# A hand-ordered gated-recurrence and feed-forward kernel: a new order, chunk 3 transposed by DMA, the last output tile in halves

## The chip, the cores and the metric

The kernel runs on one core of a Trainium2 chip. The metric is the device time of one execution in microseconds (us), and the verdict compares medians of repeated runs. Beside the times there is one profiled execution, whose trace says for each instruction when it ran and what it had waited for. The engines are named as in the profile: PE (TensorE: matmuls; its weight loads are PEld), DVE (VectorE), ACT (ScalarE), POOL (GpSimd) and SP (SyncE, which here only issues DMAs).

## The reference

Two layers are computed one after the other. The first is a gated recurrence over 768 steps, for 4 batches and 8 heads of width 48:

```
f = 1 / (1 + exp(-f_logit))
for t in range(S):
    state = f[:, :, t, :, None] * state + einsum('bhd,bhde->bhde', k[:, :, t], v[:, :, t])
    y[:, :, t] = einsum('bhd,bhde->bhe', q[:, :, t], state)
```

Its output, as 3072 tokens of width 384 (8 heads by 48), goes through a feed-forward layer with 2048 hidden columns:

```
h = x @ w_in
g = h + sin(alpha * h)**2 / (alpha + 1e-9)
out = g @ w_out
```

Inputs and output are float32. The kernel does its matmuls in bfloat16.

## The kernel before

**Tiling.** The 768 steps are cut into 6 chunks of 128. In a chunk the recurrence becomes matmuls. Cumulative sums of the logarithm of f come from a matmul with a triangular mask (line 311), and ACT turns them into the factors `G` and `Gi`. DVE or POOL multiply q and k by these into a tile `qk` (line 329). The tile is transposed into `tr`, so that a 128x128 product of k and q can be made for each head (`a_`, line 368). DVE applies the triangular mask (line 372), and two sets of matmuls, with the carried state (`inter_`, line 378) and with v (`intra_`, line 384), give the chunk's y. The state for the next chunk is made by `kv_` (lines 400 and 402) and a multiplication (line 413). `attend(c, b)` does this for one chunk and one batch, 24 times in all.

**Two ways to transpose.** For chunks below `PE_TR` the tile `qk` is transposed by PE: eight matmuls with the identity into a PSUM bank (line 361, two steps of four), and one copy of 1024 columns to SBUF (line 421) on DVE or ACT. For the others SP issues one DMA transpose (line 424). Likewise y becomes the feed-forward's input `xT` by PE (line 392) and a copy (line 395) for chunks below `Y_TR`, and by a DMA transpose (line 440) for the others. `PE_TR` is 4 and `Y_TR` is 3.

**Feed-forward.** In `first` (line 474; `first_half`, line 493, for chunk 0) PE multiplies two 128-column blocks of `w_in` by a chunk's 512 tokens. ACT takes the sine (line 459), and DVE adds it to h (line 462) into `g`. `second` does one tile of 128 tokens by 384 output columns: 16 accumulating matmuls (line 506, in eight steps of two), one copy from PSUM (line 512) and one store of 192 KB (line 515). Both weight matrices are loaded as float32 in pieces of 768 KB (lines 251 and 271) and scaled by alpha into bfloat16 (lines 257, 276 and 278). The scale for `w_in` is spread over the partitions by PE in float32 (line 254).

**The order.** Every step is an `op` with the engines that may do it, a cost for each, and the steps it depends on. The costs play no part when the program is built: what decides is the list `ORDER`, which was planned beforehand. Each entry is a number that packs three things: the step (`x % 2000`), the engine among those allowed (`x // 2000 % 5`), and the PSUM bank (`x // 10000`).

```
for nth, x in enumerate(ORDER):
    o = ops[x % 2000]
    ...
    yield o, list(o.engs)[x // 2000 % 5]
```

Each engine runs its own instructions strictly in the order of this list. SP too: a DMA whose data are not ready keeps back all the DMAs behind it. The SBUF buffers of each kind (`SLOTS`) are handed out in the same order.

Of the kernel before, what the change touches and what calls it, by code (L numbers as in the profile page):

```python
# [18 lines left out]
ORDER = [6, 133, 134, 0, 2, 10136, 70, 137, 7, 20142, 139, 138, 143, 145, 144, 8, 2147, 3, 30050, 71, 10079, 81,  # L19
    40148, 20160, 1, 146, 161, 73, 80, 140, 149, 2084, 82, 74, 4, 162, 75, 60163, 2083, 20097, 76, 164, 10, 9,  # L20
    5, 98, 2150, 2077, 151, 99, 196, 40085, 14, 60100, 197, 86, 20199, 152, 2087, 101, 2135, 170, 2078, 50205,
    10153, 154, 51, 171, 40165, 2141, 2072, 60088, 155, 57, 166, 200, 201, 2204, 20107, 206, 207, 156, 10102,
    103, 54, 2167, 89, 40168, 50090, 237, 2157, 91, 60095, 12, 238, 70158, 104, 169, 108, 10056, 40105, 2092,
    2106, 240, 20246, 241, 50093, 2094, 159, 242, 247, 52, 70053, 30172, 58, 2210, 2209, 173, 96, 40112, 113,
    2203, 55, 174, 50187, 109, 10059, 114, 60, 60118, 188, 11, 248, 2251, 70184, 30175, 176, 15, 189, 202, 119,
    40121, 208, 185, 20115, 50181, 61, 177, 120, 10211, 16, 62, 212, 110, 30178, 60224, 225, 186, 17, 64, 70190,
    249, 116, 2213, 2250, 122, 111, 214, 191, 117, 182, 243, 226, 66, 20265, 266, 215, 2244, 60130, 2267, 183,
    252, 2239, 2063, 123, 68, 192, 10124, 40268, 18, 269, 253, 20127, 70193, 40270, 125, 271, 179, 22, 50748,
    254, 272, 126, 768, 273, 2065, 749, 769, 10758, 759, 245, 13, 40738, 739, 180, 30274, 131, 770, 67, 771,
    740, 760, 761, 762, 275, 763, 772, 128, 129, 69, 773, 132, 194, 2198, 20227, 195, 741, 742, 743, 764, 19,  # L30
    750, 228, 744, 745, 310, 765, 60255, 774, 20, 311, 26, 751, 20319, 25, 353, 354, 2766, 320, 746, 747, 30362,
    752, 775, 363, 40216, 217, 256, 10356, 322, 218, 60257, 219, 70229, 230, 753, 776, 231, 21, 321, 2323, 258,
    259, 2324, 20276, 277, 358, 40220, 357, 2260, 23, 232, 10313, 2312, 754, 755, 364, 261, 60235, 221, 24,
    70233, 262, 20339, 30222, 33, 2355, 234, 236, 27, 314, 756, 315, 428, 40263, 290, 291, 60294, 264, 340, 757,
    223, 359, 429, 318, 295, 40286, 287, 341, 292, 365, 296, 20278, 30, 279, 28, 293, 297, 282, 288, 283, 289,
    280, 60298, 284, 2360, 281, 299, 285, 300, 40306, 307, 20302, 303, 788, 10379, 789, 790, 791, 792, 301, 308,
    304, 309, 2367, 469, 60798, 799, 2366, 70382, 34, 40431, 433, 383, 305, 2317, 32, 50437, 20342, 380, 384,
    2361, 343, 800, 316, 438, 10368, 369, 370, 793, 794, 70393, 795, 432, 381, 40325, 439, 42, 2471, 801, 470,
    394, 31, 2796, 20385, 50344, 797, 37, 38, 434, 2436, 345, 10478, 395, 2442, 2435, 346, 326, 480, 479, 386,
    70778, 2347, 472, 473, 474, 779, 20371, 542, 440, 327, 29, 780, 802, 803, 2441, 40328, 767, 10443, 444, 373,  # L40
    372, 329, 543, 20330, 35, 2476, 804, 445, 781, 482, 30336, 374, 375, 2376, 40387, 41, 805, 2806, 807, 337,
    331, 332, 50350, 36, 10456, 545, 457, 388, 2333, 546, 389, 60377, 351, 390, 20446, 447, 782, 481, 483, 378,
    475, 46, 783, 784, 2458, 50507, 40808, 809, 547, 10551, 497, 498, 20459, 352, 60484, 2544, 485, 648, 785,
    810, 579, 508, 338, 2430, 460, 2499, 50334, 811, 812, 20500, 649, 486, 461, 2786, 2335, 462, 553, 813, 501,
    60448, 552, 463, 2464, 449, 70391, 40, 450, 50348, 814, 20487, 10502, 503, 349, 815, 2392, 451, 554, 50466,
    489, 43, 504, 580, 488, 60408, 787, 409, 2505, 816, 548, 777, 467, 509, 555, 490, 550, 20400, 2477, 410,
    40424, 491, 492, 401, 425, 411, 396, 397, 60404, 402, 405, 426, 403, 427, 398, 20416, 2549, 417, 493, 406,
    399, 40412, 413, 420, 421, 418, 407, 60828, 829, 830, 831, 568, 419, 414, 422, 415, 70838, 20656, 423, 452,
    506, 39, 30588, 40453, 50582, 590, 589, 454, 657, 592, 839, 840, 677, 841, 583, 658, 465, 832, 569, 833,
    842, 570, 468, 30494, 495, 843, 40571, 44, 2593, 817, 844, 845, 455, 846, 522, 584, 572, 573, 2496, 20514,  # L50
    515, 557, 847, 516, 523, 50848, 574, 47, 659, 70565, 849, 850, 2591, 586, 524, 851, 2585, 566, 517, 678,
    40576, 2581, 2660, 2587, 852, 853, 854, 834, 70651, 525, 855, 653, 2655, 835, 20818, 856, 2836, 30680, 558,
    594, 2556, 577, 681, 652, 819, 682, 820, 821, 822, 40595, 605, 60685, 70560, 559, 561, 562, 563, 686, 823,
    824, 567, 2654, 596, 825, 687, 48, 2689, 2826, 837, 606, 607, 45, 564, 60530, 531, 532, 20518, 519, 40510,
    511, 608, 688, 669, 609, 698, 610, 10597, 533, 520, 521, 857, 512, 598, 49, 2611, 599, 513, 2600, 601,
    60526, 527, 528, 575, 20613, 30602, 614, 538, 539, 529, 2650, 578, 540, 603, 40858, 859, 615, 50868, 869,
    870, 60534, 535, 871, 683, 872, 873, 661, 541, 860, 861, 2684, 2679, 20699, 878, 879, 536, 537, 880, 881,
    690, 612, 882, 883, 60670, 884, 885, 2886, 874, 10701, 700, 862, 702, 703, 604, 875, 20662, 671, 60620, 827,
    876, 2704, 691, 692, 50672, 673, 674, 863, 621, 2675, 622, 864, 663, 705, 865, 623, 50693, 616, 617, 676,
    694, 618, 695, 20632, 60664, 665, 2866, 696, 633, 70888, 889, 634, 619, 635, 40624, 625, 626, 644, 645, 890,  # L60
    891, 646, 20628, 627, 629, 647, 892, 40636, 666, 630, 697, 893, 894, 867, 2667, 895, 637, 898, 899, 631,
    10918, 638, 20640, 919, 668, 896, 639, 920, 641, 642, 643, 60706, 40714, 715, 900, 901, 902, 877, 20710,
    903, 904, 711, 905, 716, 717, 921, 922, 906, 923, 924, 925, 897, 712, 907, 713, 40718, 707, 908, 2926, 909,
    719, 20730, 708, 720, 910, 911, 709, 731, 10928, 721, 929, 930, 931, 932, 933, 934, 935, 936, 937, 60968,
    732, 733, 969, 970, 40722, 723, 724, 971, 725, 70958, 20726, 727, 887, 927, 728, 912, 913, 914, 40734, 959,
    960, 735, 729, 736, 737, 915, 10938, 20948, 949, 961, 2916, 950, 951, 952, 953, 954, 955, 956, 957, 972,
# [42 lines left out]
def kernel(  # L109
# [66 lines left out]
    def at(b):  # L176
        return T[b.ring][b.place]
# [166 lines left out]
    def attend(c, b):  # L344
# [84 lines left out]
        if not first:  # L429
            last_ = op({PE: 170}, inter_, deps=[a, made["st", c - 1, b]], takes=[yb], holds=[trb, sold])  # L430
# [149 lines left out]
```

## Time and profile before

| | |
|---|---|
| median of 4 runs | 194.16 us (193.87 to 194.5) |
| the profiled execution's own time | 194.26 us |
| its span, first to last instruction | 192.5 us |
| PE busy | 178.9 us (93%), 1545 matmuls |
| PE weight loads | 106.7 us (55%) |
| DVE busy | 135.8 us (71%) |
| ACT busy | 125.8 us (65%) |
| POOL busy | 63.7 us (33%) |
| mean granted PE clock | 0.952 of full speed |
| HBM read and written | 25.18 MB and 4.72 MB |

The span is 1.8 us shorter than the profiled execution's time; the rest lies before the first and after the last instruction. The busy time of PE counts a matmul from its start to its modelled end, and neighbouring matmuls overlap. How long one really occupies the array is read from the distance between the starts of neighbours. The row PEclk of the page gives the clock that the throttle granted in each fortieth of the span.

### The profile page before, as it was taken

To read this page: it belongs to the slowest core of one execution; us is meant where nothing else is said; L and a number is where in the kernel's file an instruction comes from. 1 tells how busy PE (TensorE), PEld (TensorE's weight loads), DVE (VectorE), ACT (ScalarE), POOL (GpSimd) and SP (SyncE) were. 2 spreads that over 40 slices of the span, in tenths; PEclk is the share of its full clock that TensorE was granted. 3 is DMA by queue.
4 is the path that set the end of the run, shared out by engine and by line. 5 is a ranking of instruction groups with operands and counts; after the bars stand their busy time and mean duration, and the time that the engine had idled before them with its cause. 6 is when DMAs were issued, how large, how long until landed. Compare 5 with 4: busy or idle time off the path is not lost.

```text
span 192.5 us, 3900 instructions
## 1 busy us (share of the span) xinstructions
PE 178.9 (93%) x1545; PEld 106.7 (55%) x1545; DVE 135.8 (71%) x171; ACT 125.8 (65%) x184; POOL 63.7 (33%) x92
## 2 busy tenths in 40 slices
PE   0687999999999899999989999999999999999992
PEld 0254746787567446677744555555555454555561
DVE  3067796599977699889889979789549764455420
ACT  2957775799787979778887888686225554442401
POOL 4277204760014295886560071565300000000000
PEclk9997555999999999999999999999999999999998
DMA  6999999989999999999999689968711130103023
GB/s 134 223 218 217 309 301 277 251 202 327 251 205 209 230 224 240 181 252 200 252 197 219 138 189 206 227 130 181 151 43 25 58 95 11 41 0 123 3 82 123
DMA packets 119732, 33.43 MB, mean 174 GB/s; under 512 B 113041, under 2 KB 118177, under 8 KB 119713
## 3 DMA queue, kind: packets, MB, share of 16 engines
q1 hardware_dynamic: 119680, 33.17, 80.2%
q8 instruction: 12, 0.20, 0.4%
q14 instruction: 6, 0.05, 0.1%
q10 hardware_dynamic: 34, 0.02, 0.0%
HBM read 25.18 MB, written 4.72 MB: 155 GB/s over the span
## 4 chain that ended last, share of the span: by engine, by line
PE 74%; DMA 11%; SPq 6%; DVE 3%; ACT 3%; issue 1%; POOL 0%; ACTq 0%; DVEq 0%
PE banks L506 29%; PE banks L474 24%; PE banks L493 6%; SPq L219 6%; DMA f<-in_f_logit_dram 3%; DMA v<-in_v_dram 3%; PE banks L254 3%; PE banks L368 3%; DMA out_dram<-osb 3%; DMA q<-in_q_dram 3%; PE banks L384 2%; PE banks L311 2%; PE banks L402 2%; PE banks L378 1%; PE banks L361 1%
## 5 line engine op out<-in xcount | busy, mean ns | idle before, releaser
L506 PE MATMUL banks<-w_out_bf,g 128*128 128x384 bf16 x384 | 72.4, 326 | 0.0
L462 DVE SCALAR_TENSOR_TENSOR g<-s,banks 128x1024 bf16<-128x1024 f32 (+1 forms) x56 | 57.9, 1063 | 16.9 <-ACT s L459 16.8
L459 ACT ACTIVATE s<-banks 128x1024 f32<-128x1024 f32 (+1 forms) x56 | 49.4, 903 | 31.1 <-PE banks L474 27.2
L474 PE MATMUL banks<-xT,w_in_bf 128*128 128x512 bf16 x240 | 57.1, 379 | 1.2 <-DVE yn L388 0.6
L506 PEld LDWEIGHTS <-g 128*128 128x128 bf16 x384 | 35.0, 98 | 23.0
L474 PEld LDWEIGHTS <-w_in_bf 128*128 128x128 bf16 x240 | 22.6, 98 | 25.0 <-issue 1.7
L372 DVE TENSOR_TENSOR at<-banks,mask 128x1024 bf16<-128x1024 f32 x24 | 29.1, 1221 | 6.3 <-PE banks L368 4.6
L329 POOL TENSOR_TENSOR qk<-q,G 128x384 bf16<-128x384 f32 x18 | 18.3, 1022 | 19.3 <-DMA q<-in_q_dram 13.3
L329 POOL TENSOR_TENSOR qk<-k,Gi 128x384 bf16<-128x384 f32 x21 | 21.1, 1016 | 9.8 <-DMA k<-in_k_dram 7.5
L297 POOL CAST vb<-v 128x768 bf16<-128x768 f32 x12 | 9.8, 823 | 23.8 <-DMA v<-in_v_dram 23.8
L290 ACT ACTIVATE f<-f 128x768 f32<-128x768 f32 x12 | 10.2, 848 | 7.0 <-DMA f<-in_f_logit_dram 6.9
L548 ACT ACT_TABLE_LOAD x11 | 14.1, 1283 | 0.2
L493 PE MATMUL banks<-xT,w_in_bf 128*128 128x256 bf16 x96 | 14.2, 309 | 0.0
L512 DVE COPY osb<-banks 128x384 f32<-128x384 f32 x12 | 6.7, 555 | 10.2 <-PE banks L506 7.8
L512 ACT COPY osb<-banks 128x384 f32<-128x384 f32 x12 | 5.7, 475 | 12.4 <-PE banks L506 12.4
L361 PE MATMUL banks<-ident,qk 128*128 128x128 bf16 x128 | 12.0, 233 | 2.0 <-POOL qk L329 1.8
L319 ACT ACTIVATE G<-banks 128x388 f32<-128x388 f32 (+1 forms) x24 | 11.8, 499 | 2.7 <-PE banks L314 1.9
L322 ACT ACTIVATE Gi<-banks 128x384 f32<-128x384 f32 x24 | 11.4, 492 | 2.3 <-PE banks L311 1.1
L493 PEld LDWEIGHTS <-w_in_bf 128*128 128x128 bf16 x96 | 10.2, 110 | 4.5 <-DVE w_in_bf L257 1.5
L413 POOL TENSOR_TENSOR st<-sum,gl 128x384 bf16<-128x384 f32 x11 | 9.4, 858 | 5.5 <-DVE sum L410 5.5
L311 PE MATMUL banks<-lf,mask 128*128 128x384 bf16 x24 | 8.9, 383 | 2.2 <-ACT lf L293 2.2
L361 PEld LDWEIGHTS <-qk 128*128 128x128 bf16 x128 | 8.5, 103 | 4.2 <-POOL qk L329 2.6
(55 smaller groups left out, 175.5 us busy)
## 6 DMA issues: line engine op xcount, KB each, us to landing
f<-in_f_logit_dram SPq DMA_DIRECT2D x12, 384.0 KB, 5.8
k<-in_k_dram SPq DMA_DIRECT2D x12, 384.0 KB, 5.4
q<-in_q_dram SPq DMA_DIRECT2D x12, 384.0 KB, 5.6
v<-in_v_dram SPq DMA_DIRECT2D x12, 384.0 KB, 5.8
out_dram<-osb SPq DMA_DIRECT2D x24, 192.0 KB, 2.1
wst<-in_moe_w_in_dram SPq DMA_DIRECT2D x4, 768.0 KB, 7.2
wst<-in_moe_w_out_dram SPq DMA_DIRECT2D x4, 768.0 KB, 6.8
xT<-yn SPq DMA_TRANSPOSE x12, 2.4
```

The source lines that it names most:

```text
L311: nc.tensor.matmul(cs[:, :H * D].rearrange("c (p r d) -> c p r d", r=2, d=D), mask, at(lf)[:, :, i, :, :D], start=True, stop=True)
L319: nc.scalar.activation(out=at(Gb)[:, :n_G], in_=ps(cb, n_G), func=Act.Exp, scale=-1.0)
L329: engine[e].tensor_mul(at(qkb)[:, j, :, :, :D], at(src)[:, i * H:(i + 1) * H, :].rearrange("c (r p) d -> c p r d", r=2), g.rearrange("c (p ...
L361: nc.tensor.transpose(ps(tpb, 1024, BF16)[:, (j * HP + p) * C:(j * HP + p + 1) * C], at(qkb)[:, j, p, :, :].rearrange("c r e -> c (r e)"), ...
L372: nc.vector.tensor_mul(at(atb), ps(ab, 1024).rearrange("c (r p t) -> c r p t", r=2, p=HP), mask4.unsqueeze(1).to_broadcast([C, 2, HP, C]))
L459: nc.scalar.activation(out=at(sb)[:, :n], in_=ps(hb, n), func=Act.Sin, bias=QUARTER)
L462: nc.vector.scalar_tensor_tensor(take(at(gb)), at(sb)[:, :n].rearrange("p (j t) -> p j t", j=2), -1.0, ps(hb, n).rearrange("p (j t) -> p j ...
L474: nc.tensor.matmul(ps(hb, 2 * TOK)[:, j * TOK:(j + 1) * TOK], w_in_bf[:, kb, f * P:(f + 1) * P], at(xb)[:, :, kb, :], start=(kb == 0), sto ...
L493: nc.tensor.matmul(h[:, j, :], w_in_bf[:, kb, (fb + j) * P:(fb + j + 1) * P], at(xb)[:, ts, kb, :], start=(kb == 0), stop=(kb == KB - 1))
L506: nc.tensor.matmul(ps(ob, d_model), at(bufs["g", c, fb])[:, j - fb, t * P:(t + 1) * P], w_out_bf[:, j, :], start=(j == 0), stop=(j == FB - 1))
L512: (nc.scalar.copy if e == ACT else nc.vector.tensor_copy)(at(sbuf), ps(ob, d_model))
L548: nc.scalar.preload_act_table_set(now)
```

## The change

Four things are changed.

1. `ORDER` is another list: all engines run the same kinds of steps in another order, partly on other engines and in other PSUM banks.
2. `PE_TR` goes from 4 to 3, so that the four `qk` tiles of chunk 3 are transposed by DMA.
3. `second` splits the very last tile (chunk 5, batch 3) into two halves of 192 output columns. Each has its own accumulation, copy and store. The new function `columns` holds what `second` held.
4. Costs in the `op` calls are altered (for instance 310 to 225 for `a_`, 2050 to 2500 for a weight load, 1700 to 1400 and 1000 to 500 for the DMA transposes). They describe what the new list was planned with; no instruction depends on them.

```diff
-ORDER = [6, 133, 134, 0, 2, 10136, 70, 137, 7, 20142, 139, 138, 143, 145, 144, 8, 2147, 3, 30050, 71, 10079, 81,
...
+ORDER = [2, 70, 71, 60073, 70079, 6, 40000, 133, 80, 74, 1, 3, 2082, 81, 4, 2076, 50059, 134, 70136, 75, 137,
...
-PE_TR, Y_TR, SUM = 4, 3, 2
+PE_TR, Y_TR, SUM = 3, 3, 2
...
-        l = op({SP: 500}, ld, takes=[b], dma=2050)
+        l = op({SP: 500}, ld, takes=[b], dma=2500)
...
-        a = op({PE: 310}, a_, deps=[tr], takes=[ab], holds=[trb])
+        a = op({PE: 225}, a_, deps=[tr], takes=[ab], holds=[trb])
...
     def second(c, t):
+        last = (c, t) == (NCH - 1, B - 1)
+        for ms in [slice(0, d_model // 2), slice(d_model // 2, d_model)] if last else [slice(0, d_model)]:
+            columns(c, t, ms, ms.stop - ms.start)
+
+    def columns(c, t, ms, n):
         ob, sbuf = Buf("ps"), Buf("osb")
         prev = None
         for fb in range(0, FB, 2):
             def mm(e, fb=fb):
                 for j in (fb, fb + 1):
-                    nc.tensor.matmul(ps(ob, d_model), at(bufs["g", c, fb])[:, j - fb, t * P:(t + 1) * P], w_out_bf[:, j, :],
+                    nc.tensor.matmul(ps(ob, n), at(bufs["g", c, fb])[:, j - fb, t * P:(t + 1) * P], w_out_bf[:, j, ms],
                                      start=(j == 0), stop=(j == FB - 1))
...
-            (nc.scalar.copy if e == ACT else nc.vector.tensor_copy)(at(sbuf), ps(ob, d_model))
+            (nc.scalar.copy if e == ACT else nc.vector.tensor_copy)(at(sbuf)[:, :n], ps(ob, n))
...
-            nc.sync.dma_start(out=out[t * S + c * C:t * S + (c + 1) * C, :], in_=at(sbuf))
+            nc.sync.dma_start(out=out[t * S + c * C:t * S + (c + 1) * C, ms], in_=at(sbuf)[:, :n])
```

## The prediction

> **What bounds the kernel now.** I read the page's busy times and slices first, then the table of stretches, then PE's timeline, then the chain.
>
> ```profile
> PE 178.9 (93%) x1545; PEld 106.7 (55%) x1545; DVE 135.8 (71%) x171; ACT 125.8 (65%) x184; POOL 63.7 (33%) x92
> ...
> PE   0687999999999899999989999999999999999992
> ...
> PEclk9997555999999999999999999999999999999998
> ```
>
> PE is the full engine, and its granted clock is half for three slices and part of a fourth. The table of stretches (PE, PEld, DVE, ACT and POOL busy, then clock, DMA share, GB/s) gives the edges:
>
> ```profile
> 17.10:34.20 17.10, 16.52 (x118) 10.11 (x117) 12.97 (x15) 11.93 (x22) 4.24 (x8) 0.50 1.09 284
> 34.20:46.40 12.20, 11.86 (x132) 9.59 (x131) 10.23 (x14) 10.98 (x19) 6.78 (x8) 1.00 1.01 267
> 46.40:102.00 55.60, 54.44 (x596) 34.14 (x595) 47.37 (x64) 45.73 (x70) 28.74 (x36) 1.00 1.14 222
> 102.00:142.00 40.00, 40.00 (x329) 22.06 (x328) 33.23 (x38) 27.16 (x37) 14.75 (x18) 1.00 0.82 171
> 142.00:189.20 47.20, 47.14 (x299) 25.43 (x298) 25.43 (x25) 19.26 (x23) 0.00 (x0) 1.00 0.16 51
> ```
>
> From 34.2 to 189.2 PE is idle for about 1.6 us in all (12.20-11.86, 55.60-54.44, 47.20-47.14). So the end is set by three things: how much PE has to stream, how long it streams at half clock, and about 3.3 us of tail after its last matmul. The tail is in the chain: the copy starts at 189.22 and takes 0.48; the span ends at 192.5.
>
> PE's timeline (start, duration) shows the half clock and what a change of form costs:
>
> ```profile
> 26.23 2.07 PE L254 MATMUL banks<-al_row,ones_f 1*128 1x512 f32 x2
> 28.23 5.30 PE L493 MATMUL banks<-xT,w_in_bf 128*128 128x256 bf16 x24
> 33.46 1.47 PE L254 MATMUL banks<-al_row,ones_f 1*128 1x512 f32 x2
> 34.86 4.10 PE L493 MATMUL banks<-xT,w_in_bf 128*128 128x256 bf16 x36
> ...
> 51.70 0.49 PE L506 MATMUL banks<-w_out_bf,g 128*128 128x384 bf16 x2
> 52.12 0.40 PE L368 MATMUL banks<-tr 64*128 64x128 bf16 x8
> 52.45 2.77 PE L506 MATMUL banks<-w_out_bf,g 128*128 128x384 bf16 x16
> ```
>
> 24 matmuls of line 493 need 5.23 us at half clock, 36 need about 4.0 at full: 0.218 against 0.11 each. Line 368 uses 64 rows of the array, its neighbours 128. The second L506 starts at 51.86 and should occupy 0.16, to 52.02; L368 starts at 52.12, so going in costs 0.10. Its eight starts lie (0.40-0.216)/7 = 0.026 apart (0.216 is one of them alone), which makes 0.21; L506 follows after 0.33, so going out costs 0.12. One run of L368 among others thus costs about 0.2 us beyond its own streaming.
>
> **What the Trainium skill says.** "TensorE: Matmul & The Clock Gate", section "What's actually happening": the clock is set by activity in free-running windows of 3.413 us, and returns to full after a busy window. The trace agrees on the length: 17.1 us at half clock are five windows. They end at 27.4, 30.8 and 34.2, and the one from 27.4, three quarters of it dense L493, was not enough. Section "Back-to-back issue gap": N/2.4 + 2.5 ns at full clock. Agrees: L506 (N=384) takes 0.163, as 32 of them fill 5.21 us of the chain. "DMA: Bandwidth & Descriptors", section "Issuing engines are not separate DMA queues": all DMAs share 16 engines and interleave. The list of DMA issues (last number: median us from issue to landing) agrees: loads, mostly issued while the engines were full, take longer than the eight `tr` transposes, which ran from 103 to 139:
>
> ```profile
> f<-in_f_logit_dram SPq DMA_DIRECT2D x12, 384.0 KB, 5.8
> ...
> tr<-qk SPq DMA_TRANSPOSE x8, 3.2
> ```
>
> **The change part by part.**
>
> *Chunk 3 by DMA.* Four tiles of eight L361 matmuls go. The chain has eight in 0.45 us, 0.056 each: 32 x 0.056 = -1.8 us of PE, in stretches where PE never rests, so on the path. Three DVE copies (0.685) and one ACT copy (1.007) go too. Added are four transposes on SP: 1.25 us of SP's time each (the eight of before: median 1258 ns), 5 us in all, and 3.1 to 4.1 us from issue to landing. In the new order they stand near together on SP, with one load between, ahead of f, k and v loads for the next chunk; these wait behind them if a `qk` is late. The bounds: nothing, if PE reaches `a_` later than the landing, to 5.8 - 3.2 = 2.6 us per wait if transposes in the crowded stretch land as late as loads.
>
> *Fewer changes of form.* The order of PE's instructions has the 192 L368 in 24 runs before and 17 after; chunk 0's four stay separate in both. 7 x 0.2 = -1.4 us, on the path. Bounds 1.3 and 1.6.
>
> *The start.* The first 17 DMAs on SP are the same but for one exchange: f of the fourth half-chunk now goes ahead of v of the second, which so lands some 1.8 us later than its 19.1, at about 20.9, and its cast ends near 21.7. PE has a 2.0 us L254, two L311 and others between, and reaches that v only near 23: hidden; with no cover it costs 1.8. Then comes the gain. Before, PE did an L254 (26.23 to 28.23) between the last y transpose and the first L493. After, L493 follows at once, needing `w_in_bf`, whose first fold ran 24.16 to 25.9 on DVE, and x. PE gets there near 26.4, still cold, and then has 24 L493 in a row, to 31.6. The window 27.4 to 30.8 is then dense throughout, and the clock should rise at 30.8, not 34.2: 3.41 x 1/2 = -1.7 us. With windows elsewhere in phase the dense 5.2 us still covers most of one, so -0.5 to -2.5; 0 if DVE keeps PE from using it. DVE is the cover that may be missing. Its row, with 1.75 a fold and 0.6 a sum (line 462): second fold to 28.5, three sums from 29.2, third fold once its L254 is through (32.3) to 34.0, a fourth sum, fourth fold to 36.3, six sums and an `st` to 40.4, the first `w_out` fold to 42.1, a sum to 42.7. PE's first L506 needs the last two: about 43, against 46.39. I take -1.6. A check: before, 142.8 us passed from the first L506 to the last matmul's end; counts times spacings give 1.3 less of PE work behind that point after, and with the 0.7 below the last matmul ends at 43 + 142.8 - 1.3 + 0.7 = 185.2, 4.0 earlier.
>
> *The last tile in halves.* 32 matmuls of 192 columns at (192/2.4 + 2.5) = 82.5 ns for 16 at 162.5: +0.05. The last copy is 192 columns: ACT takes 0.475 for 384 and 0.602 for 512, so 0.32 for 192: -0.15. The store is 96 KB for 192 KB. The last one before ran from 189.72 to its landing at 191.58; half the bytes save 0 to 0.35, I take 0.2. Sum -0.3.
>
> *Work moved between engines.* The order gives DVE 3 more `gl` (0.48), 2 more `qk` products (0.7), 3 more `st` (0.55) and 2 more `yn` (0.55), one `xT` less (0.35) and the 3 copies less: +3.2 us. ACT loses 1.3, POOL 5.5. DVE is busy 80.6 of the 95.6 us from 46.4 to 142, and 83.8 would still fit under PE. Without that cover it costs up to 3.2.
>
> *New waits.* Before has 1.6 us of PE idleness from 34.2 on, which the new order needn't repeat or keep. I take the same and 0.7 more, for DMA transposes and loads in the crowded stretch: bounds -1.2 and +8.
>
> Sum: -1.8 - 1.4 - 1.6 - 0.3 + 0.7 = -4.4. The profiled execution took 194.26 us (span 192.5), so 189.9; it lies 0.1 above the median of 194.16, hence 189.8. No difference under about 0.2% (0.4 us) can be told from no change.
>
> **The rivals.**
>
> *A. Part of it is given back.* PE's savings of 3.2 and the tail stand, but the clock rises in the same window as before, or DVE's 3.2 us come into the open, or a load is late. For: DVE and ACT are 85% and 82% busy in 46 to 102, and in the chain of before they and DMA waits appear between 83 and 101. Against: PE was idle for only 1.2 us there. With no gain at the start and 1.5 us of new waits: 194.2 - 3.5 + 1.5 = 192.2.
>
> *B. Slower: SP's queue.* The place is chunk 3, where PE reaches three of the four `a_` within 0.7 us of its own work and the fourth 4.5 us later. If the transposes land like loads, at 5.8 and not 3.2, PE stands twice for 2.6, and the loads for chunk 4 are issued 5 us later, a further wait of up to 5 when they are needed: +10. For: the stretch's DMA share is full, and a load of f from 83.52 that took 6.63 us and a q of 4.82 at 93.63 are links of the chain. Against: from 102 to 142 twenty transposes shared the queue with loads and PE was busy for 40.00 of 40.00. It decides once waits exceed 5.1 us; at 6.5 the time is 195.6.
>
> *C. The change does nothing to be seen.* That needs the waits to match 5.1 by chance.
>
> **How the numbers follow.** The forecast as summed 0.56, A 0.26, B 0.14, C 0.04. Forecast and A are faster: 0.82; same 0.04; slower 0.14. The forecast's own range is 188 to 191.3: the start at -2.5 and no new wait gives 188.2, the start at 0 gives 191.4. The range reaches over A: 187.8 to 193.8, with B and little else outside.
>
> **What would show it.** Right: 96 L361; the half-clock stretch ending at least one window earlier; the first L506 near 43; PE idle under 2.5 us from there to its end; the last matmul near 185; 3.0 us behind it. Wrong: PE waiting at line 368 for `tr` by DMA, or at line 474 or 493 for DVE; loads of chunk 4 late behind line 424's DMAs; or a half clock up to 34 us and beyond.

## The result: a little slower, and where the time went

The kernel after the change takes 195.08 us (median of 33 runs, 193.23 to 197.88), beside 194.25 us for the kernel before (54 runs). The ratio is 1.0031, 95% interval 1.0011 to 1.005. The forecast was 189.8. Medians here are of all executions, while the ratios leave out those more than 1.5% above the fastest of the same kernel, so a ratio can lie below that of the medians. The profiled execution of the changed kernel took 196.73 us (span 195.0), 1.6 us above its own median, so its losses are somewhat larger than those of a typical one. The lines after 500 have moved by five: line 506 is now 511, line 512 is 517, line 515 is 520.

The page of the kernel after, busy times and slices:

```profile
PE 176.3 (90%) x1529; PEld 106.5 (55%) x1529; DVE 139.2 (71%) x177; ACT 124.5 (64%) x183; POOL 59.7 (31%) x84
...
PE   0676989988999999999999929999999999999993
...
PEclk9996559999999999999999985999999999999998
DMA  6999999979899999899999939959895320100222
```

PE is busy 2.6 us less (178.9 before), and the half clock of the start ends a slice earlier. But in slice 24 of the 40 PE is 20% busy, and in slices 24 and 25 of its clock row (8 and 5) a second stretch of half clock stands, which the kernel before does not have. The table of stretches (columns as in the prediction) puts edges to it:

```profile
16.47:30.12 13.65, 12.29 (x111) 8.20 (x109) 10.10 (x13) 9.69 (x17) 2.24 (x5) 0.50 1.04 272
30.12:44.45 14.33, 13.08 (x115) 9.91 (x113) 12.65 (x15) 11.77 (x19) 7.91 (x8) 1.00 1.01 268
44.45:113.20 68.75, 68.51 (x709) 42.34 (x708) 60.38 (x77) 58.09 (x89) 29.08 (x38) 1.00 1.04 214
113.20:117.20 4.00, 0.09 (x4) 0.07 (x2) 0.84 (x2) 0.91 (x1) 1.78 (x2) 0.78 0.25 50
117.20:142.00 24.80, 24.80 (x187) 13.04 (x188) 18.07 (x20) 13.15 (x19) 11.40 (x13) 0.90 0.95 189
142.00:191.65 49.65, 49.41 (x345) 28.27 (x344) 28.92 (x31) 20.86 (x25) 2.48 (x3) 1.00 0.27 74
```

Between 44.45 and 113.2 us PE rests for 0.24 us; then it stands for four. PE's timeline names what it waited for (the bracket holds the idle time and what ended it):

```profile
26.81 4.38 PE L493 MATMUL banks<-xT,w_in_bf 128*128 128x256 bf16 x24 [0.41 <-ACT xT L395]
...
44.45 1.14 PE L511 MATMUL banks<-w_out_bf,g 128*128 128x384 bf16 x6 [0.95 <-DVE g L462]
...
112.99 0.26 PE L384 MATMUL banks<-vb,at 128*128 128x48 bf16 x4
117.16 1.44 PE L474 MATMUL banks<-xT,w_in_bf 128*128 128x512 bf16 x3 [3.91 <-DMA xT<-yn]
```

It is the first matmul of chunk 3's feed-forward, waiting for that chunk's y, which line 440 transposes by DMA. The clock records show half clock from 115.46 to 122.28, two windows; the 5.12 us of it in which PE worked cost 2.56. By the distance of the starts, less what the matmul before needs, the wait is 4.07 us; wait and clock together are 6.6 us. From there the balance closes. The first line-511 matmul starts 1.94 us earlier than before (44.45 for 46.39), what lies behind the last matmul's start is 0.39 shorter (3.34 for 3.73), and what lies between grows by 4.78 (147.20 for 142.42). The sum is the 2.5 us by which the span grew. Of the 4.78, +6.6 are wait and clock. The rest is -1.8: by the two tables of stretches, some 0.7 of it is short idleness of before that did not recur (1.2 us between 46.4 and 189.2 before, 0.5 between 44.45 and 191.65 now, the long wait apart), and some 1.1 is PE's lighter work.

Why the y transposes were late is read from two timelines of the kernel after. ACT makes the first of chunk 3's four y tiles:

```profile
102.75 0.48 ACT L388 CAST yn<-banks 128x384 bf16<-128x384 f32 x1 [0.41 <-PE banks L384]
```

SP issues its DMAs in the same stretch:

```profile
101.91 2.97 SPq L219 DMA_DIRECT2D v<-in_v_dram  x1
104.96 1.45 SPq L520 DMA_DIRECT2D out_dram<-osb  x1
106.51 1.26 SPq L424 DMA_TRANSPOSE tr<-qk  x1
107.82 0.57 SPq L219 DMA_DIRECT2D q<-in_q_dram  x1
108.44 7.53 SPq L440 DMA_TRANSPOSE xT<-yn  x4
```

The first y was ready at 103.23, and its transpose was issued at 108.44: a load of v held for 2.97 us, a store, a transpose of chunk 4 and a load of q stood ahead of it. The last of the four y's was ready at 107.64 and its transpose issued at 114.73; it landed at 117.07, 0.09 us before PE went on. In the kernel before, the same four were issued from 102.21 to 108.26 and had landed by 111.79, for a need at 113.82:

```profile
102.21 1.40 SPq L440 DMA_TRANSPOSE xT<-yn  x1
...
105.02 2.56 SPq L440 DMA_TRANSPOSE xT<-yn  x2
...
108.26 2.06 SPq L440 DMA_TRANSPOSE xT<-yn  x1
```

But they did not stand shorter in SP's queue there. The first and the last y of chunk 3 in the kernel before, and the last in the kernel after, are made here:

```profile
94.14 0.48 ACT L388 CAST yn<-banks 128x384 bf16<-128x384 f32 x1
100.57 0.55 DVE L388 CAST yn<-banks 128x384 bf16<-128x384 f32 x1
...
107.17 0.47 ACT L388 CAST yn<-banks 128x384 bf16<-128x384 f32 x1
```

From ready to issue, the first y took 7.6 us before and 5.2 after, the last 7.1 in both. What differs is when the y's are made. The new list puts chunk 2's 48 matmuls of line 474 (from 84.81 us) ahead of chunk 3's `a_` (from 98.19); in the kernel before these `a_` (from 87.45) came ahead of that block (from 96.28). PE was hardly idle up to 113.2 us, so this is the list and not a delay. The last y is ready 6.5 us later than before, for a need that comes 0.6 us earlier. From the last y to PE's need the old list has 12.7 us and the new one 5.6. Standing in the queue and landing took 10.7 us before and 9.4 after: it fits into the first and not into the second.

SP is behind in the loads too. By 100 us it has issued 42 loads of q, k, v and f before, and 38 after (with four transposes more); the last of the 48 lands at 134.16 before, at 143.07 after.

### The profile page after: what moved, and what is told of

Its sections match the earlier page's. It is cut to its first block, busy times and chain, and to the rows that moved or that the text cites. A ratio compares the mean times of both kernels' runs of the same rounds, so it can differ in the third digit from the quotient of the medians.

```text
span 195.0 us, 3886 instructions
## 1 busy us (share of the span) xinstructions
PE 176.3 (90%) x1529; PEld 106.5 (55%) x1529; DVE 139.2 (71%) x177; ACT 124.5 (64%) x183; POOL 59.7 (31%) x84
## 3 DMA queue, kind: packets, MB, share of 16 engines
q1 hardware_dynamic: 124048, 34.22, 80.3%
## 4 chain that ended last, share of the span: by engine, by line
PE 76%; SPq 7%; DMA 7%; DVE 4%; ACT 3%; issue 2%; POOL 0%; DVEq 0%
PE banks L511 31%; PE banks L474 25%; SPq L219 5%; PE banks L493 5%; PE banks L368 3%; PE banks L384 3%; DMA v<-in_v_dram 3%; DMA out_dram<-osb 3%; PE banks L254 2%; PE banks L311 2%; PE banks L378 2%; DVE g L462 2%; PE banks L402 2%; DVE w_out_bf L278 1%; SPq L440 1%
## 5 line engine op out<-in xcount | busy, mean ns | idle before, releaser
L511 PE MATMUL banks<-w_out_bf,g 128*128 128x384 bf16 (+1 forms) x400 | 72.5, 320 | 1.0 <-DVE g L462 1.0
L474 PE MATMUL banks<-xT,w_in_bf 128*128 128x512 bf16 x240 | 57.7, 389 | 4.4 <-DMA xT<-yn 3.9
L511 PEld LDWEIGHTS <-g 128*128 128x128 bf16 x400 | 35.9, 98 | 22.2 <-issue 1.7
L329 POOL TENSOR_TENSOR qk<-q,G 128x384 bf16<-128x384 f32 x19 | 19.0, 1006 | 37.1 <-ACT G L319 16.6
L329 POOL TENSOR_TENSOR qk<-k,Gi 128x384 bf16<-128x384 f32 x18 | 18.1, 1017 | 11.2 <-DMA k<-in_k_dram 10.5
L517 ACT COPY osb<-banks 128x384 f32<-128x384 f32 (+1 forms) x13 | 5.9, 456 | 16.8 <-PE banks L511 15.1
L493 PE MATMUL banks<-xT,w_in_bf 128*128 128x256 bf16 x96 | 13.1, 296 | 0.7 <-ACT xT L395 0.4
L388 DVE CAST yn<-banks 128x384 bf16<-128x384 f32 x13 | 7.1, 554 | 6.7 <-PE banks L384 6.7
L384 PE MATMUL banks<-vb,at 128*128 128x48 bf16 x192 | 10.8, 189 | 0.7 <-POOL vb L297 0.7
L384 PEld LDWEIGHTS <-at 128*128 128x128 bf16 x192 | 9.0, 101 | 3.2 <-issue 1.6
```

The lines of the kernel that those rows point to most:

```text
L329: engine[e].tensor_mul(at(qkb)[:, j, :, :, :D], at(src)[:, i * H:(i + 1) * H, :].rearrange("c (r p) d -> c p r d", r=2), g.rearrange("c (p ...
L384: nc.tensor.matmul(ps(yb, H * D)[:, h * D:(h + 1) * D], at(atb)[:, r, p, :], at(vb)[:, i, h, :], start=(first and p == r == 0), stop=(r == ...
L474: nc.tensor.matmul(ps(hb, 2 * TOK)[:, j * TOK:(j + 1) * TOK], w_in_bf[:, kb, f * P:(f + 1) * P], at(xb)[:, :, kb, :], start=(kb == 0), sto ...
L493: nc.tensor.matmul(h[:, j, :], w_in_bf[:, kb, (fb + j) * P:(fb + j + 1) * P], at(xb)[:, ts, kb, :], start=(kb == 0), stop=(kb == KB - 1))
L511: nc.tensor.matmul(ps(ob, n), at(bufs["g", c, fb])[:, j - fb, t * P:(t + 1) * P], w_out_bf[:, j, ms], start=(j == 0), stop=(j == FB - 1))
L517: (nc.scalar.copy if e == ACT else nc.vector.tensor_copy)(at(sbuf)[:, :n], ps(ob, n))
```

## The experiments

The first question was whether that one wait is the loss. **Theory 1** says yes: take it away, and the time falls to about 190. (Theory 2, in two of the expectations, says that other limits stand right behind it.) It fell, and **theory 3** took its place: the stream of loads, stores and transposes through SP and the 16 DMA engines is a second limit close behind PE's. (From 80 to 130 us these engines are busy 0.86 or more of every 10 us in the kernel before, and 0.96 or more in the kernel after but for the 10 us with the wait.) Whatever PE gains, it spends in waiting for the next item of that stream, and the four new transposes make the stream longer. Every ratio below is to the kernel before, run beside it on the same chip.

### The kernel after, once more

No edit.

> The changed kernel unaltered, for a second trace and as the yardstick of this call. If the profiled execution was typical, PE waits 3 to 5 us before its first line-474 matmul of chunk 3 for the DMA transposes of y, and the time is 194.5 to 195.6 us; if that wait was an accident of one execution, it is under 1 us here and the time is the same all the same.

195.22 us (22 runs), ratio 1.0024 [0.9995, 1.0053]. Its profile has the same wait (4.11 us, from 113.64) and the same two windows of half clock (116.12 to 122.94); but this execution took 197.87 us, 2.65 above the median, so no profile shows a typical execution. For those there are the recorded mean clocks of 56 executions of this kernel. In 36 it is 0.991, which is one window of 3.41 us at half clock in some 190 us, in 9 about 0.98, two windows, in 5 it is 1.0. In this profile, and in seven others of the new order, the record of the clock begins at 26 to 32 us, behind the half clock of the start, so that such figures leave it out. The mean does not say where the window lies, and the kernel before has 0.991 too (15 of 59 executions beside this run). But in the four kernels below that have the same start and a much shorter wait, 0.991 stands in 1 of 37 executions. So a later half clock most likely belongs to most executions of the changed kernel, and is mostly one window.

### The y transposes earlier on SP

```diff
-... 2449, 40492, ... 460, 486, 813, 814, 20770, 771, 2464, 2497, 2540, 40, ... 817, 450, 501, ...
+... 2449, 450, 40492, ... 460, 486, 461, 487, 813, 814, 20770, 771, 2464, 2497, 498, 40, 41, 799, 2540, ...
```

The steps 450, 461, 487 and 498 are the four y transposes; 40 and 41 are loads of q and v, 799 is a store.

> Only SP's order differs from the changed kernel: the four transposes of chunk 3's y go directly behind the steps that make y, ahead of one q load, one v load (which lands 14 us before it is used) and one store. Theory 1, the wait for those transposes and the half clock after it ate the gain: the wait of 4.1 us falls below 1 us, the clock stays full, and the time is 188.5 to 191.5 us. Theory 2, other limits (DVE, the g buffers, loads) stand right behind: the wait moves elsewhere and the time stays within 1 us of 195.

194.92 us (22 runs), 0.9987 [0.9956, 1.0017]. The waits of PE in its profile (us in total, times, longest; line 473 is 474):

```profile
PE banks L473 <- DVE osb L516: 2.5, 1, 2.5
PE banks L473 <- DMA xT<-yn: 2.2, 1, 2.2
```

Chunk 3's y transposes landed by 111.44 now, and PE began its feed-forward at 113.09 without a wait. The first of the two waits is another: 2.63 us from start to start, at 114.64, for a PSUM bank that DVE had yet to copy out (lines 516 and 519 are 517 and 520):

```profile
116.82 0.56 DVE L516 COPY osb<-banks 128x384 f32<-128x384 f32 x1 [4.61 <-DMA out_dram<-osb]
...
112.97 1.69 SPq L519 DMA_DIRECT2D out_dram<-osb  x1
```

DVE stood for 4.61 us until the store that was moved back (799), issued at 112.97, had landed at 116.73 and freed its `osb` buffer. The second wait is new too: chunk 4's y transposes, at 145.64, where the kernel after had lost 0.41 a little later. The four were moved up; what had stood ahead of them is late now.

### Other work of PE in the gap

```diff
-... 778, 564, 40530, 565, 531, 489, ...
+... 778, 564, 836, 837, 60840, 841, 842, 843, 844, 845, 846, 847, 40530, 565, 531, 489, 558, ...
```

Ten steps of output tiles (3.25 us) are moved ahead of chunk 3's first matmul, and DVE's step 558 a little forward. One of the tiles is begun in bank 6 before chunk 3's `kv` of one batch has been read from there, so the state of that batch is not the reference's; no instruction is left out.

> Only PE's order differs from the changed kernel: ten steps of line 511 (3.25 us of work on chunk 2, ready long before) go ahead of the first line-474 matmul of chunk 3, and one DVE addition goes ahead of two others. The DMAs keep their order. Theory 1: PE works where it waited, the remaining wait is about 1 us, too short for the clock to fall, and the time is 189.5 to 192. Theory 2: the ten steps are missed later, as cover for sine and addition of chunk 3, and the time stays within 1 us of 195.

195.04 us (22 runs), 0.998 [0.9952, 1.0009]. The wait at 113 us is gone and PE's clock stays full. Its profile's waits (lines 367 and 473 are 368 and 474):

```profile
PE banks L367 <- DMA tr<-qk: 2.0, 1, 2.0
PE banks L473 <- DMA xT<-yn: 1.8, 1, 1.8
```

They lie at 133.84 and 144.41: chunk 4's `qk` and y. Two edits of different engines take the wait for chunk 3's y away, and both times PE waits at another place instead, for something that came through SP: a store's buffer or a later transpose. Theory 1 has fallen.

### Half the bytes, in both kernels

In chunks 3 to 5 each load of f, k, q and v brings half of its rows; the number and the order of the DMAs stay.

```diff
         def emit(e):
-            engine[e].dma_start(out=at(b), in_=srcs[n][bp * 2 * H:(bp + 1) * 2 * H, c * C:(c + 1) * C, :]
+            h = H if u >= 6 else 2 * H
+            engine[e].dma_start(out=at(b)[:, :h], in_=srcs[n][bp * 2 * H:bp * 2 * H + h, c * C:(c + 1) * C, :]
```

> The kernel after, with each load of chunks 3, 4 and 5 (24 of the 48) carrying half of its rows, so half of the bytes; the other half of these tiles keeps what an earlier chunk left there, and the output of chunks 3 to 5 is not the reference's. The order and every other instruction stay. It tells the bytes from the issues: if the DMA engines' work is the limit (theory 3a), the loads land early, SP's issues that were held 2 to 3 us take under 1 us, the waits ahead of the y transposes vanish with the half clock, and the time is 188.5 to 191. If SP's own issue time of the transposes and the order are the limit (theory 3b), or the waits are those for producers on ACT and DVE, the wait keeps 2 us or more and the time is 193.5 to 195.5.

> The kernel before, with the loads of chunks 3, 4 and 5 cut to half of their rows (half of their bytes), as was done to the kernel after; the output of chunks 3 to 5 is not the reference's. The control of that run. Theory 3 (the stream of loads, stores and transposes is a limit that only the changed kernel runs into; before loses 0.8 and 0.7 us to waits after 60 us and none of them to a DMA): 192.5 to 194.5, so that the changed kernel with half the bytes, 191.4, stands 1.5 to 3 us under it, which is what the change gains on TensorE. Rival (half the bytes would help any of these kernels by 3 to 4 us): 190 to 191.5.

The changed kernel with half the bytes takes 191.4 us (6 runs), 0.9829 [0.9777, 0.9882]: 3.8 less than the changed kernel. The kernel before with half the bytes takes 193.65 (15 runs), 0.9967 [0.9944, 0.999]: 0.6 less. The same relief is worth six times as much to the changed kernel, and with it the change is a gain of 2.2 us by the medians (2.7 by the ratios; the two were measured at different times). In the profile of the changed kernel so relieved, SP's timeline has the four y transposes:

```profile
105.98 5.18 SPq L440 DMA_TRANSPOSE xT<-yn  x4
```

and PE's the wait for them:

```profile
114.26 0.81 PE L474 MATMUL banks<-xT,w_in_bf 128*128 128x512 bf16 x3 [1.05 <-issue]
```

Four issues take 5.18 us for 7.53 and begin 2.46 earlier; 1.05 of the 3.91 us remains, and the clock stays full. The last y was ready at 107.60, as in the kernel after; it is the standing in the queue that has shrunk.

### Late stores, in both kernels

```diff
-SLOTS = dict(... osb=3, ...)
+SLOTS = dict(... osb=15, ...)
...
+    T["osb"] += [t[:, i * d_model:(i + 1) * d_model] for t in T["wst"] for i in range(4)]
```

In `ORDER` 13 stores (11 in the kernel before) are moved behind the last DMA transpose. The weights' staging buffers are read for the last time at about 52 us and hold the waiting tiles (three `osb` tiles are made as before, the other twelve are slices). Nothing is left out.

> The kernel after, with 13 of its 25 stores moved on SP behind the last transpose by DMA (some 150 us); the evicted tiles are kept until then in 12 more osb buffers, which lie in the staging buffers of the weights, unused after 51 us. Nothing is left out and no other instruction moves. Some 8 stores of 192 KB leave the stream ahead of 130 us: 1.6 MB at 0.2 MB a us is up to 7 us of the stream, and 0.4 to 2.8 us of SP each. Theory 3: the waits for chunk 3's y transposes and the half clock behind them shrink or go: 189.5 to 192.5. Rival (SP is late for what ACT and POOL produce, and stores are not in its way): 194 to 196.

> The kernel before with the same late stores: 11 stores moved on SP behind its last transpose by DMA, kept in 12 more osb buffers inside the weights' staging buffers. The control of the late stores. Theory 3 (only the changed kernel runs into the stream): 193.2 to 194.6, as half the bytes gave 193.65. Rival (late stores help any order of this kernel by 2 us or more, and the change itself is worth nothing even without the limit): 191 to 192.5.

The changed kernel with late stores takes 191.72 us (6 runs), 0.9849 [0.9796, 0.9901], the fastest here that computes the whole. The kernel before with late stores takes 193.49 (22 runs), 0.9955 [0.9933, 0.9977]. So 3.4 us for the one and 0.7 for the other, as with half the bytes. PE at the place of the wait, in the changed kernel with late stores (line 473 is 474):

```profile
112.82 0.81 PE L473 MATMUL banks<-xT,w_in_bf 128*128 128x512 bf16 x3 [1.64 <-DMA xT<-yn]
```

1.64 us are left of 3.91, another 1.4 stand at 142 us (chunk 4's y), and five of the six executions have no half clock on record. The edit does two things, later stores and more `osb` buffers; which of them counts was not parted.

### Chunk 3 by DMA, alone

```diff
-PE_TR, Y_TR, SUM = 4, 3, 2
+PE_TR, Y_TR, SUM = 3, 3, 2
-... 435, ... 443, 444, 445, ... 456, 457, ... 2458, ...
+... 2435, 443, ... 372, 454, ... 471, 480, ... 477, 491, ...
```

The kernel before; each of the four groups of transpose, transpose, copy is replaced by one DMA transpose (443, 454, 480 and 491; later steps are renumbered).

> The kernel before, with one part of the change alone: chunk 3's q and k are transposed by DMA, each issue placed on SP where its q or k is ready (one of them behind the next free tr buffer); the order is otherwise that of before. Theory 3: PE saves 1.8 us and up to 0.7 us of form changes, but SP's later issues move by up to 5 us; the y transposes of chunk 3, which landed 2 to 3 us early, land about 2 us too late, and the half clock may return: 194 to 197. Rival (the four transposes by DMA are harmless, the new order did it): the saving is kept, 191.5 to 193.

204.18 us (6 runs), 1.0485 [1.0426, 1.0544]: ten us slower, far beyond what either theory said. PE's timeline (lines 366, 390 and 504 are 368, 392 and 506):

```profile
85.97 0.33 PE L390 MATMUL banks<-ident,yn 128*128 128x128 bf16 x3
90.74 0.40 PE L366 MATMUL banks<-tr 64*128 64x128 bf16 x8 [4.45 <-DMA tr<-qk]
...
96.02 0.81 PE L504 MATMUL banks<-w_out_bf,g 128*128 128x384 bf16 x4
100.90 0.40 PE L366 MATMUL banks<-tr 64*128 64x128 bf16 x8 [4.07 <-DMA tr<-qk]
```

These are the two waits at `a_` that rival B had priced at 2.6 each, and each has a window of half clock at it (91.35 to 94.77 and 101.59 to 105.0). The four `qk` themselves were early. In the kernel before, a chunk 3 `qk` is ready 5.9 to 7.5 us before its `a_` (the first at 81.52 for 87.45), and PE's transposes and the copy fit in between. By DMA the tile of the first wait was ready at 81.12, was issued at 85.13 behind loads and a store, and landed at 90.69, 5.6 us later (rival B had feared 5.8); that of the second was ready at 85.91, issued at 96.81, landed at 100.86. So 9.6 and 14.9 us went by from ready to landed, of which 4.0 and 10.9 were standing in SP's queue. The same kernel with late stores was to tell whether the crowded stream makes it so:

> The kernel before with chunk 3's q and k transposed by DMA (204.2) and the late stores. If the crowded stream makes those transposes late, the waits of 4.5 and 4.1 us ahead of the 64-row products shrink by half or more and the time is 196 to 200. If the old order leaves too little time between q and k and their use whatever the stream does (an issue of 1.25 us and 3 to 4 us to land), the waits stay above 3 us each and the time is 202 to 205.

203.73 us (6 runs), 1.0484 [1.0454, 1.0514]: nothing gained; its two waits are 4.97 and 3.97 us. So the stores were not in the way at this place. What stood ahead of the second tile here (ready 87.12, issued 96.93) were loads and two other transposes, which the edit leaves where they are. The expectation's second branch, too little time in the old order, is met in its number; but the time was short because of the place on SP that the edit gave the transposes, and no run tried another. The changed kernel's own list gives `a_` the time: three of chunk 3's `a_` follow each other from 98.19 us without a wait, and the four transposes landed by 99.90, ahead of each one's use.

### Chunk 3 back on PE, in the new order

```diff
-PE_TR, Y_TR, SUM = 3, 3, 2
+PE_TR, Y_TR, SUM = 4, 3, 2
-... 427, 822, 791, 792, 793, 794, 443, 795, 455, 410, 491, 40481, 411, ...
+... 427, 830, 410, 411, 443, 444, 445, 10456, 457, 2458, 40484, 485, 486, 50497, 498, 499, 799, 800, 801, 802, 803, ...
```

That is the last of three placements (its expectation calls it the second); steps are renumbered by the eight that come in, so that 822 is 830 and 791 is 799. Two further output steps (804 and 805) come a little earlier as cover for PE, so it is not the bare undoing. A first one put two of the transposes into banks 0 and 1 ahead of the snake step (sine and addition) that reads them, so chunk 2's hidden values are partly overwritten there.

> The changed kernel with chunk 3's qk transposed by PE again (PE_TR 4): 32 PE transposes (+1.8 us) and four copies back, four DMA transposes (5 us of SP's time) gone, everything else in the new order. If these four DMAs crowd SP's queue and so delay the transposes of y: the wait at chunk 3 falls below 1 us and the time is 190.5 to 193. If the queue is late for its loads and order alone: a wait of 2 us or more stays and the time is 195 to 197.

199.42 us (6 runs), 1.0234 [1.0189, 1.0278]; its profile has waits of 3.00 and 1.58 us at the new transposes and behind their copies, released by DVE, which the placement made itself, and it tells nothing on the question. In the second placement the banks were free:

> The kernel after, with one part undone: chunk 3's q and k are transposed on TensorE again (four pairs of transposes and four evictions put back where banks 0, 1, 4 and 5 are free in its order, at about 95 us), the rest of the new order kept, SP's too. It tells whether the four transposes by DMA are what makes SP and the DMA stream late. Theory 3 (the stream of loads, stores and transposes is a second limit and the four transposes, some 1.25 us of SP each, push what stands behind them by about 5 us): PE pays 1.8 us of transposes and about 0.7 us of form changes back, the 4.1 us wait ahead of chunk 3's first matmul shrinks under 1.5 us, the half clock behind it (2.5 us) goes, and the time is 191 to 193. Rival (the new order of the loads, stores and y transposes on SP is late by itself): the wait stays at 2 us or more or moves on to chunks 4 and 5, and the time is 195 to 197.5.

196.55 us (22 runs), 1.0066 [1.0038, 1.0095], where theory 3 said 191 to 193. The reason is again one of placement. SP's waits in this profile (line 218 is 219, line 292 is 293):

```profile
SPq L218 <- ACT lf L292: 10.5, 1, 10.5
```

Two of the copies stood on ACT ahead of a Sin, so ACT's next Exp began at 101.83 instead of 97.70. The load of f that needs that buffer waited, and kept back all of SP for 10.5 us. Together with the earlier y transposes of the second experiment it was worse still:

> The run before this one (chunk 3's q and k on TensorE again) together with SP's issues of chunk 3's y transposes placed right behind their y copies, ahead of a load of q, a load of v and a store. Theory 3: with the stream relieved, the earlier y transposes take away what is left of the wait and nothing moves on to chunks 4 and 5: 190.5 to 192, faster than the kernel before by 1% or more. Rival (the order on SP is late by itself, whatever is queued first): the wait moves to chunks 4 and 5 at 2 us each, and the time stays at 194.5 to 197.

199.9 us (6 runs, 196.66 to 202.24), 1.0173 [1.0088, 1.0257], a ratio that rests on two executions only. The profiled execution (202.24 us) has a wait of 3.48 us at 120.6, one of 1.91 at 101, and a window of half clock at each. The long one is that of the second experiment again: DVE's copy of an output tile began at 123.64, when the store that was moved back had landed (123.54) and freed its buffer. In the third placement the copies come behind the Sin:

> The kernel after, chunk 3's q and k transposed on TensorE again, in a second placement: the copies behind ACT's and DVE's snake steps and not ahead of them (in the first placement an Exp of ACT came 4 us late, and with it a load of f that waits for its buffer), and seven products moved up as cover. Theory 3: the four transposes gone from the stream give back some 2 us of it and 5 us of SP; the wait for chunk 3's y transposes falls under 2 us without half clock, TensorE pays 1.8 to 2.5 us: 191.5 to 194. Rival (the order of SP is late by itself): 195 to 197.

> The two runs before this one together: chunk 3's q and k transposed on TensorE in the second placement, and 13 stores moved behind the last transpose by DMA. Theory 3: with both, the stream is relieved by 9 us and no wait for a DMA above 0.5 us remains, but TensorE keeps its 1.8 to 2.5 us: 190.5 to 192.5, near or above the late stores alone. Rival: no better than the placement on TensorE alone, 194 to 197.

193.43 us (19 runs), 0.9935 [0.9909, 0.9962], and with late stores 191.98 (6 runs), 0.9881 [0.9844, 0.9918]. So against this placement, chunk 3 by DMA costs 1.7 to 1.9 us net in the new order (a ratio of 1.0024 or 1.0031 for 0.9935), though it takes 1.8 us of transposes off PE; against the second placement (196.55) it gains some 1 us. With the stream relieved the two ways can't be told apart, 191.72 and 191.98 with intervals that overlap. In the third placement 1.5 us of wait for chunk 3's y is left (113.28), and 0.6 and 1.3 us at chunk 5's `qk` and chunk 4's y, so waits for DMAs are still left there.

## Why the prediction was wrong, step by step

*What bounds the kernel.* PE's stream, its clock and its tail were named as the only three things. That is right of the kernel before, and both controls bear it out: half the bytes and late stores gain it 0.6 and 0.7 us. But the column of the DMA share stood in the same table, 1.14 in 46.4 to 102 us, and it was read as a price for single transposes and not as a second limit with its own sum. The page's share of the DMA queue is that sum: 80.2% of 192.5 us before, 154.4 us of all 16 engines, and for the kernel after:

```profile
q1 hardware_dynamic: 124048, 34.22, 80.3%
```

That is 80.3% of 195.0, 156.6 us: the four transposes and what came with them add some 2 us to a stream that has to be through before chunk 5's attention can end, while PE was to come 3 to 4 us earlier to it.

*Chunk 3 by DMA, -1.8.* The PE side was right: 96 matmuls of line 361. Landing in the crowded stretch was put at 3.2 to 5.8 us; the `tr` of the kernel after land after 3.1 to 4.5, median 3.5:

```profile
tr<-qk SPq DMA_TRANSPOSE x12, 3.5
xT<-yn SPq DMA_TRANSPOSE x12, 2.3
```

That loads take longer to land than transposes was taken as agreement with DMAs that share their engines; the two differ in size (384 KB and 256 KB) and in where they read, so it does not test this. The runs do: with half the bytes in the loads alone, the y transposes' four issues took 5.18 us for 7.53.

*Fewer changes of form, -1.4, and the work behind the first line-506 matmul, -1.3 in all.* Measured -1.8 with the wait and the clock taken out, of which some 0.7 is idleness of before that didn't recur, so about -1.1. The size fits, and the 24 and 17 runs of line 368 are as counted; no run did the changes of form alone.

*The start, -1.6.* The clock's part came as forecast: the half clock lasted 13.65 us for 17.1, one window less, and the clock was full from 30.12 (30.8 predicted). But the first line-511 matmul, forecast 3.4 us earlier than before (43 for 46.39), came 1.94 earlier, at 44.45, so 1.45 us of the forecast was lost. The gap is DVE's: the first `w_out` fold began at 41.44, where the forecast had 40.4, and took 2.37 us, against 1.75 for a fold of the same kind, and PE's first line-511 matmul waited 0.95 us for the sum behind it. What stood beside the longer fold is told in the last section.

*The tail, -0.3.* Measured -0.39. The last copy, ACT at 191.94, took 0.32 as predicted:

```profile
191.94 0.32 ACT L517 COPY osb<-banks 128x192 f32<-128x192 f32 x1 [1.28 <-PE banks L511]
```

*Work moved between engines, 0.* DVE's 3.4 us more (139.2 for 135.8) stayed under PE but for the 0.95 us just named: it released no longer wait of PE in this profile.

*New waits, +0.7.* This is the step that failed. It measured 4.07 us of wait and 2.56 of half clock in the profiled execution, and the runs with late stores and half the bytes give back 3.4 and 3.8 us in the medians. Three things were missed in it. The wait was looked for at the transposes that the change adds, and not at others on the same queue: I counted 5 us of SP's time, and named only loads for chunk 4 as what comes later. The room for chunk 3's y transposes was not read from the new list, which leaves 5.6 us from the last y to its use for 12.7 in the old. And the wait was priced at its own length, while the half clock behind it cost 2.56 us here, and would cost up to 1.7 where it is one window. Against this one term, the others together were less far off: the savings came to some 4.2 us (1.94, 1.8 and 0.39, that idleness included) where 5.1 were forecast.

*Rival B* had the mechanism, SP's queue, with a chance of 0.14, and the side of the result. Its place was wrong for this kernel: `a_` did not wait, the y transposes of line 440 did, where the kernel before was busy for 40.00 of 40.00 us. That place would have been right had the old order been kept, where the two waits are 4.45 and 4.07. Its "against", twenty transposes that had cost nothing from 102 us on (sixteen of them were issued by 142 us, the other four later), counted on slack in the old order (2.0 us from landing to need for chunk 3's y), which the new list did not keep. *Rival A*, a part given back, was the right kind of case with the wrong ceiling: what was given back was more than all of the savings. The forecast itself came true only with the stream relieved, and then by half: -2.2 us with half the bytes and -1.8 with late stores, each against the kernel before relieved in the same way.

**What stays open.** What the runs show is that relief of SP's queue gives the loss back to the changed kernel and hardly anything to the kernel before. Two things are in that loss, a longer stream and a list that makes chunk 3's y's later. Taking the four transposes off the stream gave back 1.7 us (the third placement, whose last y is ready at 107.85, as late as in the kernel after); no run changed the second alone. That the sum of the stream is a limit by itself is an inference too: its share is no hard ceiling (it reaches 1.14), and in the kernel before it is 0.79 from 130 to 140 us. The order of `ORDER` is a plan of nearly a thousand steps, and no run shows how much of the loss a better list with the same four transposes would avoid without moving stores. The bytes and SP's time for issuing were not fully parted: half the bytes shortens both, since a held issue is shorter when the engines are free.

## What to carry to other kernels

Where the trace shows two resources nearly full, sum both before you price a saving on one: here the engine had 178.9 of 192.5 us and the DMA stream 154.4, packed into the first 140, and the forecast saving on the engine came out, by half, only when the stream was relieved. When work is moved to a DMA queue, look for the loss at whatever is queued behind it and needed soonest. Take as the room for it the time from ready to use in the new order, less the standing in the queue that the old trace shows (7 us here), not the slack in the old trace. What is pushed back to make room has a deadline too, if its buffer is needed again: the store behind the y transposes stopped a copy, and the copy stopped PE. Before giving up such a change, look for transfers without a deadline: moving 13 stores back turned it from 0.3% slower to 1.5% faster than the kernel before.

## What was not expected of the hardware

The transpose of a `qk` tile by DMA takes about 3 us from issue to landing even where the stream is relieved: 3.0, 3.3 and 4.0 us (least, median, most) with half the bytes, 3.1, 3.5 and 4.5 in the kernel after. Most of that time is its own and not the crowd's, though single ones took up to 5.6 (chunk 3 by DMA in the old order); what the crowd mostly adds is the standing in SP's queue ahead of the issue.

A wait of PE can be followed by a half clock that outlasts it, and its length alone does not tell: 3.91 us of idleness brought two windows (6.83 us), 4.45 and 4.07 one window each, and in the second placement on PE even a wait of 1.91 us (from 99.85) one, from 102.22 to 105.63, while waits of 2.63 us (at 114.64, the y transposes earlier on SP) and 2.09 (at 144.41, other work in the gap) brought none.

The same DVE operation, a fold of 128x1536 from float32 to bfloat16, took 1.75 us in most places and 2.37 at 41.44 us in the kernel after. The traces show what stood beside it, one line of DVE and two of POOL:

```profile
41.44 2.37 DVE L278 TENSOR_TENSOR w_out_bf<-wst,al_r 128x1536 bf16<-128x1536 f32 x1
...
41.19 1.00 POOL L329 TENSOR_TENSOR qk<-q,G 128x384 bf16<-128x384 f32 x1 [3.15 <-DMA q<-in_q_dram]
42.15 1.72 POOL L325 TENSOR_TENSOR gl<-G,bd 128x8 f32<-128x8 f32 x1
```

A product of POOL was running when the fold began, and the fold ended 1.6 us after that product. The next operation of POOL, a `gl` that mostly takes 0.20 us, ended with the fold. So it looks as if one stands while the other works. Five more runs of the new order have this fold at 2.03 to 2.46 us, each time with a POOL product running at its begin and an end about 1.6 us behind it. Where the fold began first it took 1.75 and the product stood: 2.59 us for 1.00 with late stores (40.39). The folds of `w_in` (line 257), which read the scale from PSUM, took 1.75 us beside POOL products of 1.00 (34.99 in the kernel after): neither was longer there. No run changed this alone.
